# Products of the identity into unused columns of y's bank, ahead of the turning of x in tiles 13 to 23 and ahead of the last logits

## Chip, cores, metric

The kernel runs on one core of one Trainium2 chip. The metric is the device time of one execution in microseconds (us). TensorE is called PE here, VectorE DVE, ScalarE ACT, GpSimd POOL, and SyncE SP.

## What is computed

A recurrent attention (WKV) is followed by a mixture of experts. The shapes are 4 batches, 8 heads, 768 steps, head dimension 48; then 3072 tokens of 384 numbers, 8 experts with an inner width of 1024, each token going to its best two.

```python
for t in range(S):
    cur = np.einsum('bhd,bhe->bhde', u[None] * kt, vt)
    y[:, :, t] = np.einsum('bhd,bhde->bhe', rt, state + cur)
    state = w[None, :, :, None] * state + np.einsum('bhd,bhe->bhde', kt, vt)
...
noisy_logits = x @ w_gate + np.log1p(np.exp(x @ w_noise)) * noise
top2 = np.argpartition(-noisy_logits, 2, axis=1)[:, :2]
...
h = np.maximum(x[mask] @ w1[e], 0.0)
out[mask] += top2_w[mask, k, None] * (h @ w2[e])
```

## The kernel before

**Attention.** The work is cut into 24 tiles of 128 tokens, numbered `i` = 0 to 23 (`i` = 4 x chunk + batch). All instructions of an engine run in the order in which the code writes them; the order around the change is written out by hand in the loop over tiles (L1330 to L1391). For tile `i` the loop does, among other things: `ystate(i)` opens the PSUM bank `py` and multiplies by the carried state (L532); `yout(i)` first takes the logits of tile `i-1` (L574), then the masked scores times v (L532), with the sums for the u term of the next tile in the middle (`uterm_sum`, L434, from tile `PE8` = 13 on); `xout(i)` adds y and the u term on DVE and so makes x (L561); `turn_kr(i+2)` transposes k and r two tiles ahead into the banks `KX` and `RV` (L225), ACT and DVE copy them out as `kT` (L463) and `rT` (L465); `logits_out(i-1)` copies 16 columns of logits out on ACT as `lg` (L583); `scores(i+1)` makes the scores of the next tile in `PAB` (L477), which DVE masks as `am` (L485); and `turn_x(i)` transposes x into `KX` (L225) and has ACT copy it out as `xT` (L471), from which the logits are made one tile later.

**The bank `py`.** Each tile has one PSUM bank of 512 fp32 columns, called `PB[i]`. Columns 0 to 383 hold y, the next 64 hold the logits of the tile before (`PL[i-1]`, which `lg` reads), the next 8, from `CO` = 448, hold the sums of the u term. Columns 456 to 511 are used by nobody.

**The last tile.** For `i` = 23 the loop calls `xT_first` (L1062): it transposes three gathered blocks of tokens for the first expert, two of them into `RV` and `PAB`, then calls its argument, which is `turn_x(23)`, then transposes the third block into `RT` (L1075). ACT rounds the three to `xh` (L1080). `pl_alone(23)` (L1399) makes the last logits (L574, into `pl`), and then the experts begin.

**Experts.** `p1` (L1136) multiplies the blocks by w1 in 9 products of 128x384 for each of 8 slices, writing `ph`; ACT and DVE turn `ph` into `hb`. `p2` (L1172) multiplies `hb` by w2. Routing (the choice of the two experts, lists, gathers) runs in small steps on DVE and POOL between these, from generators that the loops advance.

Of the kernel before, what the change touches and what calls it, by code (L numbers as in the profile page):

```python
# [49 lines left out]
NZ_AT = 5  # L50
CV_DVE = 8
PE8 = 13
GD = 6


@with_exitstack
def kernel(
# [14 lines left out]
    nc = tc.nc  # L72
    B, H, S, D = r.shape
# [99 lines left out]
    def load_nz(b):  # L173
        nc.sync.dma_start(nz[:, :, b, :], noise[b * S:(b + 1) * S, :].rearrange("(c p) e -> p c e", p=128))
# [11 lines left out]
    ident = const.tile([128, 128], F32, name="ident")  # L186
# [35 lines left out]
    def turn_rows(dst, o, src, base=0):  # L222
        for s in range(2):
            q = slice(base + s * 64, base + (s + 1) * 64)
            nc.tensor.transpose(dst[:, s, o:o + 64], src[q], ident[q, q])  # L225
# [4 lines left out]
    def by_row(t):  # L230
        return t.rearrange("p a (s t) -> p s a t", s=2)

    def halves_of(src, o, n):
        return src[:, :, o:o + n * 64].rearrange("p s (a t) -> p s a t", t=64)
# [78 lines left out]
    def consts_b():  # L313
        nc.gpsimd.memset(zrow, 0.0)
# [102 lines left out]
    def uterm_a(i):  # L417
        if i >= PE8:
            t = att.tile([128, 512], F32, name="rku")
            RKU[i] = t.rearrange("p (a t) -> p a t", t=128)  # L420
            for h in (slice(0, NP // 2), slice(NP // 2, NP)):
                nc.gpsimd.tensor_mul(RKU[i][:, h], rT[i][:, h], kT[i][:, h])
            return
        uterm_rk(i)
        uterm_u(i)

    CO = DM + LREP * 2 * E

    def uterm_sum(i, pyb):
        c8 = pyb[:, CO:CO + H].rearrange("p (a s) -> p a s", s=2)  # L430
        for p in range(NP):
            for q in range(2):
                qs = slice(q * 64, (q + 1) * 64)
                nc.tensor.matmul(c8[qs, p, :], RKU[i][:, p, qs], uw[:, p, :], start=False, stop=True,  # L434
                                 skip_group_check=True)
        PC[i] = pyb[:, CO:CO + H]
# [3 lines left out]
    def uterm_b(i):  # L440
        c8 = att.tile([128, H, 1], F32, name="c8", bufs=2)
        if i >= PE8:
            nc.vector.tensor_copy(c8[:, :, 0], PC[i])
# [23 lines left out]
    def turn_x(i):  # L467
        for d in range(ND):
            turn_rows(KX, XO + d * 64, X[i][:, d * 128:(d + 1) * 128])
        XT[i] = att.tile([128, ND, 128], F32, name="xT", bufs=1)  # L470
        nc.scalar.activation(by_row(XT[i]), halves_of(KX, XO, ND), AF.Copy)  # L471

    def scores(i):
        pa = PAB.rearrange("p s (a b) -> p s a b", b=128)
        for p in range(NP):
            for s in range(2):
                nc.tensor.matmul(pa[:, s, p, :], kT[i][s * 64:(s + 1) * 64, p, :],  # L477
                                 rT[i][s * 64:(s + 1) * 64, p, :], start=True, stop=True)
        PA[i] = pa
# [30 lines left out]
    def zup_p(i):  # L510
        if i in ZT:
            nc.gpsimd.tensor_mul(Z[i % B], ZT[i], w128.to_broadcast([128, NP, D]))
# [28 lines left out]
    ACC, PB = {}, {}  # L541

    def yout(i):
        c, b = divmod(i, B)
        py, acc_mm = PY[i], ACC[i]
        if i:
            logits(i - 1, not c)
        for p in range(NP):
            if p == NP // 2 and PE8 <= i + 1 < NT:
                uterm_sum(i + 1, PB[i])  # L550
            for s in range(2):
                h = 2 * p + s
                for q in range(2):
                    acc_mm(py[:, h, :], AM[i][:, s, p, :], vt[i][:, h, :], q, h == H - 1)

    def xout(i):
        c, b = divmod(i, B)
        py = PY[i]
        xr = xs[i % 4]
        x = xr[:, :DM]  # L560
        nc.vector.tensor_add(x, py.rearrange("p h d -> p (h d)"), CV[i].rearrange("p h d -> p (h d)"))  # L561
        X[i] = x

    def xstore(i):
        if i >= 0:
            nc.sync.dma_start(xd[i * 128:(i + 1) * 128, :], xs[i % 4])
# [3 lines left out]
    def logits(i, alone):  # L570
        for d in range(ND):
            for q in range(2):
                qs = slice(q * 64, (q + 1) * 64)
                nc.tensor.matmul(PL[i][qs], XT[i][:, d, qs], wg[:, d, None, :].to_broadcast([128, LREP, 2 * E]),  # L574
                                 start=alone and d == 0, stop=(d == ND - 1), skip_group_check=True)
# [98 lines left out]
    def drop(g, mm2, ej2, ijv, w_, c0, first):  # L674
# [6 lines left out]
        c = 0.1 + 0.004 * wp_  # L681
        n = GD
        parts = []
# [331 lines left out]
    def chunks(e):  # L1015
        return CHUNKS1 if e else CHUNKS0
# [4 lines left out]
    def xgather(e, ci, early_=-1):  # L1021
        for t in chunks(e)[ci]:
            n = tw(t)
            xg = moe.tile([128, XW], F32, name="xg", bufs=4)
            nc.gpsimd.indirect_dma_start(  # L1025
                out=xg[:n, :XW if e else DM], out_offset=None, in_=xd[:rows_of(early_)],
                in_offset=bass.IndirectOffsetOnAxis(ap=GR[:n, e * NJ + t:e * NJ + t + 1], axis=0))
            XG[e, t] = xg
# [33 lines left out]
    def xT_first(between):  # L1062
        xh = moe.tile([128, ND, WMAX], F32R, name="xh")
        xl = moe.tile([128, ND, WMAX], F32R, name="xl")
        XH[0, 0] = (xh, xl)
        part = lambda x, t: by_row(x[:, :, t * 128:(t + 1) * 128])
        whole = RT[:, :ND * 128].rearrange("p (d t) -> p d t", d=ND)
        ts = []
        for t, dst in zip(chunks(0)[0], (RV, PAB, None)):
            if dst is None:  # L1070
                between()
            for d in range(ND):
                xg = XG[0, t][:, d * 128:(d + 1) * 128]
                if dst is None:
                    nc.tensor.transpose(whole[:, d, :], xg, ident)  # L1075
                else:
                    turn_rows(dst, d * 64, xg)
            ts.append((t, whole, xh[:, :, t * 128:(t + 1) * 128], xl[:, :, t * 128:(t + 1) * 128]) if dst is None else
                      (t, halves_of(dst, 0, ND), part(xh, t), part(xl, t)))
            nc.scalar.activation(ts[-1][2], ts[-1][1], AF.Copy)  # L1080
        for t, x, h_, l_ in ts:
            nc.vector.tensor_sub(l_, x, h_.bitcast(F32))
# [161 lines left out]
    def steps(n):  # L1244
        for _ in range(n):
            one_step()
# [67 lines left out]
    def products(i):  # L1314
        if PE8 <= i + 1 < NT:
            uterm_a(i + 1)
        if i + 2 < NT:
            prep_k(i + 2)
        zup_p(i - 1)
        if i + 1 < min(PE8, NT):  # L1320
            uterm_a(i + 1)
# [8 lines left out]
    for i in range(NT):  # L1330
        products(i)
        if early_done and (0, 0) not in XG:
            xgather(0, 0, 0)
        if i + 5 < NT:
            load(i + 5, (0, 2))
        if NZ_AT <= i < NZ_AT + B:
            load_nz(i - NZ_AT)
        if i == B:
            consts_b()
        ystate(i)  # L1340
        if i:
            kvup(i)
        yout(i)
        if not i:
            kvup(i)
        if i + 4 < NT:
            load(i + 4, (2, 3))
        xstore(i - 1)
        zup_v(i)
        if i > 1:  # L1350
            zblock(i - 2)
        uterm_c(i, CV_EARLY, H)
        steps(2)
        tick()
        if CV_DVE < i + 1 < NT:
            uterm_b(i + 1)
        steps(1)
        xout(i)
        while i == I_EARLY and not early_done:
            rstep(1)  # L1360
            maybe_early()
        if i == I_EARLY and (0, 0) not in XG:
            xgather(0, 0, 0)
        if i == NT - 1:
            logits_out(i - 1)
            route_when_done(i - 1)
            xstore(i)
            steps(3)
            xT_first(lambda: turn_x(i))
            p1a = p1(0, 0)  # L1370
        else:
            turn_kr(i + 2)
            if i:
                logits_out(i - 1)
                route_when_done(i - 1)
            uterm_c(i + 1, 0, CV_EARLY)
            steps(1)
            scores(i + 1)
            turn_x(i)
            tick()  # L1380
            steps(1)
            mask(i + 1)
            if i + 1 <= CV_DVE:
                uterm_b(i + 1)
            steps(3)
            maybe_early()
        if i == 5:
            consts_v()
        for p, t in enumerate(W_AT0):
            if W_LD.get(i) == p or t <= i <= t + 2:  # L1390
                next(wun[p])  # L1391
# [273 lines left out]
```

## Time and profile before

| | us |
|---|---|
| median of 3 runs | 592.07 |
| the runs | 592.11, 589.45, 592.07 |
| profiled execution | 594.45 |
| its span, first to last instruction | 592.3 |
| PE busy in the span | 570.7 (96%) |
| DVE, ACT, POOL busy | 346.8, 284.8, 282.0 |

The profile is of one execution, which took 594.45 us: 592.3 us of span and 2.1 us around it. Times inside the profile count from the start of the span. The first expert product starts at 127.65 us, so the attention with its last tile is a bit over a fifth of the span. In the profile, the granted clock of PE is given as a share of full speed: 1.00 is 2.4 GHz and 0.50 is 1.2 GHz, its two levels.

### The profile page before, as it was taken

How to read it: one execution, taken by the hardware profiler on the slowest of the kernel's cores; microseconds unless marked ns; L12 is line 12 of the kernel's file. 1: busy time of each engine (PE TensorE's matmuls, PEld its weight loads, DVE VectorE, ACT ScalarE, POOL GpSimd, SP SyncE). 2: the span in 40 equal slices, each digit the busy share in tenths (PEclk: the TensorE clock that was granted, in tenths of full speed). 3: DMA queues.
4: the chain of work that ended last, by engine and by line, in shares of the span. 5: the costliest groups of instructions: out<-in, count | busy, mean ns of one | idle time of the engine just before them, and what ended most of it. 6: DMA issues, size and time to landing. Idle time of an engine off the chain costs nothing.

```text
span 592.3 us, 13907 instructions
## 1 busy us (share of the span) xinstructions
PE 570.7 (96%) x5383; PEld 544.7 (92%) x5384; DVE 346.8 (59%) x781; ACT 284.8 (48%) x714; POOL 282.0 (48%) x420
## 2 busy tenths in 40 slices
PE   8999989979979999999999999999999999999995
PEld 5899979869979999999999999999999999999995
DVE  7988889778745444546455645555464546454331
ACT  4348877832343443554445554455454454445220
POOL 8997767720426443436345443444353436333222
PEclk9999999989989999999999999999999999999998
DMA  8998999167504643675655646455756555424211
GB/s 162 196 210 190 232 224 233 54 168 225 157 2 140 208 145 92 177 181 146 122 166 142 191 107 185 120 178 111 177 132 152 150 149 171 128 92 85 66 35 42
DMA packets 143225, 86.53 MB, mean 146 GB/s; under 512 B 118624, under 2 KB 133215, under 8 KB 143152
## 3 DMA queue, kind: packets, MB, share of 16 engines
q1 hardware_dynamic: 132368, 56.76, 40.2%
q0 software_dynamic: 10160, 28.81, 16.3%
q8 instruction: 44, 0.72, 0.5%
q14 instruction: 29, 0.24, 0.1%
q10 hardware_dynamic: 624, 0.00, 0.1%
HBM read 58.81 MB, written 19.86 MB: 133 GB/s over the span
## 4 chain that ended last, share of the span: by engine, by line
PE 80%; DVE 7%; POOL 6%; issue 3%; ACT 2%; DMA 1%; another core or an unknown queue 1%; POOLq 0%; DVEq 0%; ACTq 0%
PE ph L1136 36%; PE pym L1172 33%; POOL kd L403 2%; PE pym L1165 2%; PE pym L1163 2%; POOL rku L411 2%; PE py L532 2%; DVE am L485 1%; POOL rku L415 1%; PE PAB L477 1%; DVE x L561 1%; PE KX L225 1%; DVE rT L465 1%; PE RT L714 1%; PE ptm L1054 1%
## 5 line engine op out<-in xcount | busy, mean ns | idle before, releaser
L1172 PE MATMUL pym<-w1h,hb 128*128 128x384 f32 x768 | 200.2, 337 | 0.0
L1142 DVE SCALAR_TENSOR_TENSOR hb<-ph,hb 128x384 fp32r<-128x384 f32 x128 | 71.2, 557 | 119.7 <-ACT ht L1140 73.6
L1172 PEld LDWEIGHTS pym<-w1h,hb 128*128 128x128 f32 x768 | 139.4, 188 | 0.2
L1136 PE MATMUL ph<-xh,w0h 128*128 128x384 f32 (+1 forms) x384 | 136.3, 355 | 0.0
L1136 PE MATMUL ph<-xh,w0l 128*128 128x384 f32 (+1 forms) x384 | 136.2, 355 | 0.0
L1136 PE MATMUL ph<-xl,w0h 128*128 128x384 f32 (+1 forms) x384 | 130.6, 354 | 0.0
L1172 PE MATMUL pym<-w1l,hb 128*128 128x384 f32 x384 | 129.2, 336 | 0.0
L1140 ACT ACTIVATE hb<-ph 128x384 fp32r<-128x384 f32 x128 | 62.9, 492 | 111.2 <-PE ph L1136 106.4
L1197 POOL DMA_INDIRECT out_dram<-ot,TK x56 | 60.0, 1071 | 100.4 <-DVE ot L1191 44.4
L1025 POOL DMA_INDIRECT xg<-xd,GR x56 | 60.9, 1088 | 53.6 <-DVE r_e L608 24.6
L1136 PEld LDWEIGHTS ph<-xh,w0h 128*128 128x128 f32 x384 | 72.9, 190 | 3.7 <-issue 0.2
L1136 PEld LDWEIGHTS ph<-xl,w0h 128*128 128x128 f32 x384 | 72.8, 190 | 3.3
L1136 PEld LDWEIGHTS ph<-xh,w0l 128*128 128x128 f32 x384 | 72.9, 190 | 3.2
L1040 POOL DMA_INDIRECT pv<-out_dram,GA x49 | 50.1, 1022 | 51.0 <-DMA out_dram<-ot,TK 38.6
L1172 PEld LDWEIGHTS pym<-w1l,hb 128*128 128x128 f32 x384 | 72.1, 188 | 0.1
L1110 ACT ACTIVATE xh<-xj 128x384 fp32r<-128x384 f32 (+1 forms) x42 | 21.2, 504 | 43.7 <-DVE xj L1108 38.3
L1180 ACT ACTIVATE ot<-pym 128x384 f32<-128x384 f32 x42 | 20.5, 487 | 41.3 <-PE pym L1172 31.7
L1111 DVE TENSOR_TENSOR xl<-xj,xh 128x384 fp32r<-128x384 f32 (+1 forms) x42 | 22.4, 534 | 24.9 <-ACT xh L1110 18.4
L1096 ACT ACTIVATE pl<-xg 128x768 uint16<-128x768 uint16 (+1 forms) x42 | 35.3, 841 | 1.6 <-DMA xd<-pl 1.5
L485 DVE TENSOR_TENSOR am<-PAB,mneg 128x512 int32<-128x512 int32 x48 | 30.8, 685 | 4.2 <-PE PAB L477 2.8
L454 ACT ACTIVATE cv<-vt,c 128x48 f32<-128x48 f32 x120 | 30.3, 326 | 0.2
L403 POOL TENSOR_TENSOR kd<-kt,tabk 128x192 f32<-128x192 f32 x46 | 28.6, 643 | 3.6 <-PE RV L225 2.4
(275 smaller groups left out, 828.2 us busy)
## 6 DMA issues: line engine op xcount, KB each, us to landing
stg<-in_moe_w_dram SPq DMA_DIRECT2D x24, 512.0 KB
stg<-in_moe_w_dram SPq DMA_DIRECT2D x32, 384.0 KB
xd<-x SPq DMA_DIRECT2D x24, 196.0 KB
rd<-in_r_dram SPq DMA_DIRECT2D x24, 192.0 KB
vt<-in_v_dram SPq DMA_DIRECT2D x24, 192.0 KB
out_dram<-ot SPq DMA_DIRECT2D x16, 288.0 KB
kt<-in_k_dram SPq DMA_DIRECT2D x23, 192.0 KB
xg<-xd,GR POOLq DMA_INDIRECT x56
```

The costliest lines, as they stand in the source:

```text
L403: nc.gpsimd.tensor_mul(KD[i][:, h], kt[i][:, h], tabk[:, h, :D])
L454: nc.scalar.activation(CV[i][:, h, :], vt[i][:, h, :], AF.Copy, scale=C8[i][:, h, :])
L485: nc.vector.tensor_tensor(am[:, :, h].bitcast(I32), pa[:, :, h].bitcast(I32), mneg[:, None].to_broadcast([128, 2, NP // 2, 128]), op=ALU.b ...
L1025: nc.gpsimd.indirect_dma_start(out=xg[:n, :XW if e else DM], out_offset=None, in_=xd[:rows_of(early_)], in_offset=bass.IndirectOffsetOnAxi ...
L1040: nc.gpsimd.indirect_dma_start(out=pv[:n], out_offset=None, in_=out, in_offset=bass.IndirectOffsetOnAxis(ap=GA[:n, e * NJ + t:e * NJ + t + ...
L1096: nc.scalar.activation(pl[:n], XG[e, t][:n, :DM].bitcast(U16).rearrange("p (d two) -> p two d", two=2), AF.Copy)
L1111: nc.vector.tensor_sub(xl, xj, xh.bitcast(F32))
L1136: nc.tensor.matmul(ph[:, :w_], a[:, d, fs], x[:, d, :w_], start=(j == 0), stop=(j == len(q) - 1))
L1140: nc.scalar.activation(h_[:, f, 0, :], ph[:, a:b], AF.Relu)
L1142: nc.vector.scalar_tensor_tensor(h_[:, f, 1, :], ph[:, a:b], 0.0, h_[:, f, 0, :].bitcast(F32), op0=ALU.max, op1=ALU.subtract)
L1172: nc.tensor.matmul(py, hb[:, f, a, hs], x[:, f, :], start=(j == 0), stop=(j == len(q) - 1))
L1197: st = nc.gpsimd.indirect_dma_start(out=out, out_offset=bass.IndirectOffsetOnAxis(ap=TK[:n, q:q + 1], axis=0), in_=ot[:n], in_offset=None, ...
```

## The change

A new function `fill(i, n)` issues `n` fp32 products with the 128x128 identity `ident` as weights and its first 56 columns as the moving operand; they write the 56 unused columns of `PB[i]`. Nobody reads them. Three fills stand ahead of `turn_x(i)` for `i` = 13 to 22, nine ahead of `turn_x(23)` and five behind it, ahead of the last block's transposes and the last logits: 44 in all.

```diff
+FILLS = (3, 9, 5)
...
+    def fill(i, n):
+        t = PB[i][:, CO + H:]
+        for _ in range(n):
+            nc.tensor.matmul(t, ident, ident[:, :t.shape[1]], start=True, stop=True, skip_group_check=True)
+
...
-            xT_first(lambda: turn_x(i))
+            xT_first(lambda: (fill(i, FILLS[1]), turn_x(i), fill(i, FILLS[2])))
             p1a = p1(0, 0)
...
             scores(i + 1)
+            if i >= PE8:
+                fill(i, FILLS[0])
             turn_x(i)
```

The line numbers of the changed file are larger by 1 from `FILLS` on and by 6 from `fill` on. On the other engines the order of instructions is the same as before.

The order on PE at tile 13 (`x_147` is its x), with the engines that each first instruction waits for, before. `DVE` stands there for x, `Activation` for an earlier instruction of ACT.

```order
L477 MATMUL PAB<-rT,kT 128x128 x8
L225 MATMUL KX<-ident,x_147 128x64 [waits DVE_49,Activation_49]
L225 MATMUL KX<-ident,x_147 128x64 x5
L532 MATMUL py<-zb_220,rT 64x96 [waits PE_49,Activation_49]
L532 MATMUL py<-zb_220,rT 64x96 x7
L495 MATMUL RV<-vt,kd_101 48x48 [waits DMAHW3_49,DVE_49]
```

And the same place now.

```order
L478 MATMUL PAB<-rT,kT 128x128 x8
L560 MATMUL py<-ident 128x56 [waits Activation_49]
L560 MATMUL py<-ident 128x56 x2
L226 MATMUL KX<-ident,x_147 128x64 x6
L533 MATMUL py<-zb_220,rT 64x96 [waits PE_49]
L533 MATMUL py<-zb_220,rT 64x96 x7
```

Three fills came in between the scores and the turning of x. The wait moved from the turning to the first fill, names ACT alone, and the turning itself waits for nothing more.

The order on PE in the last tile, before; `xg` are the gathered blocks, `x_149` is x of tile 23.

```order
L225 MATMUL PAB<-ident,xg 128x64 x5
L225 MATMUL KX<-ident,x_149 128x64 [waits DVE_49]
L225 MATMUL KX<-ident,x_149 128x64 x5
L1075 MATMUL RT<-ident,xg 128x128 [waits DMASW2_49]
L1075 MATMUL RT<-ident,xg 128x128 x2
L574 MATMUL pl<-wg,xT 64x64 [waits Activation_49]
```

And now.

```order
L226 MATMUL PAB<-ident,xg 128x64 x5
L560 MATMUL py<-ident 128x56 [waits Activation_49]
L560 MATMUL py<-ident 128x56 x8
L226 MATMUL KX<-ident,x_149 128x64 x6
L560 MATMUL py<-ident 128x56 x5
L1081 MATMUL RT<-ident,xg 128x128 [waits DMASW2_49]
L1081 MATMUL RT<-ident,xg 128x128 x2
L580 MATMUL pl<-wg,xT 64x64 [waits Activation_49]
```

Nine fills moved in ahead of the turning of the last x and took over its wait, and five stand between it and the third block.

## Rows read from the trace of the kernel before

**Rows 1.** The page, busy us of each engine, share of the span, instructions
```profile
PE 570.7 (96%) x5383; PEld 544.7 (92%) x5384; DVE 346.8 (59%) x781; ACT 284.8 (48%) x714; POOL 282.0 (48%) x420
```

**Rows 2.** Busy us by stretch, then PE's clock, DMA share, GB/s
```profile
124.60:128.00 3.40, 1.81 (x27) 1.35 (x24) 3.10 (x9) 1.89 (x6) 0.00 (x0) 1.00 0.35 70
128.00:131.40 3.40, 3.40 (x13) 3.40 (x12) 2.12 (x12) 0.51 (x2) 0.00 (x0) 0.50 0.99 272
131.40:134.80 3.40, 3.40 (x21) 3.40 (x20) 3.13 (x10) 0.99 (x2) 0.00 (x0) 0.99 0.93 290
...
169.00:172.40 3.40, 3.02 (x18) 2.81 (x18) 1.57 (x5) 1.91 (x4) 0.00 (x0) 0.50 0.00 0
```

**Rows 3.** Chain that ended last: start us, us, engine, tile, line
```profile
81.98 0.48 DVE x L561
82.59 0.40 PE KX L225 x6
...
86.37 1.71 issue
...
94.47 0.40 PE KX L225 x6
...
107.74 1.43 POOL kd L403 x2
109.21 0.34 PE KX L225 x4
...
122.01 1.29 DVE am L485 x2
...
127.72 14.38 PE ph L1136 x72
...
210.32 4.17 PE pym L1172 x24
```

**Rows 4.** Timeline, PE turning x: start us, us, instruction, [idle before]
```profile
82.59 0.40 PE L225 MATMUL KX<-ident,x 64*128 64x64 f32 x6 [0.57 <-DVE x L561]
...
94.47 0.40 PE L225 MATMUL KX<-ident,x 64*128 64x64 f32 x6 [0.31 <-DVE x L561]
...
105.69 0.40 PE L225 MATMUL KX<-ident,x 64*128 64x64 f32 x6 [0.61 <-DVE x L561]
...
120.46 0.40 PE L225 MATMUL KX<-ident,x 64*128 64x64 f32 x6 [1.13 <-DVE x L561]
...
125.79 0.40 PE L225 MATMUL KX<-ident,x 64*128 64x64 f32 x6 [1.10 <-DVE x L561]
```

**Rows 5.** Timeline, ACT copying the logits out in the same tiles
```profile
82.48 0.18 ACT L583 ACTIVATE lg<-py 128x16 f32<-128x16 f32 x1 [1.01 <-DVE x L561]
...
94.36 0.18 ACT L583 ACTIVATE lg<-py 128x16 f32<-128x16 f32 x1 [0.81 <-DVE x L561]
...
120.50 0.18 ACT L583 ACTIVATE lg<-py 128x16 f32<-128x16 f32 x1 [2.73 <-DVE x L561]
...
125.77 0.18 ACT L583 ACTIVATE lg<-py 128x16 f32<-128x16 f32 x1 [1.59 <-DVE x L561]
```

**Rows 6.** Line L583, 60 to 130 us: ACT idle before it, us, times
```profile
  DVE x L561: 8.6, 8
```

**Rows 7.** PE by line and shape, 124.6 to 127.66 us: busy us, mean ns
```profile
L574 PE MATMUL pl<-wg,xT 128*64 128x64 f32 x12 | 0.6, 230 | 0.5 <-ACT xT L471 0.5
```

**Rows 8.** Timeline of the last tile, PE and ACT
```profile
126.12 0.55 PE L1075 MATMUL RT<-ident,xg 128*128 128x128 f32 x3
...
126.59 0.51 ACT L471 ACTIVATE xT<-KX 128x384 f32<-128x384 f32 x1
...
126.96 0.52 ACT L1080 ACTIVATE xh<-RT 128x384 fp32r<-128x384 f32 x1
...
127.15 0.57 PE L574 MATMUL pl<-wg,xT 128*64 128x64 f32 x12 [0.49 <-ACT xT L471]
...
127.65 0.44 PE L1136 MATMUL ph<-xh,w0h 128*128 128x384 f32 x1
```

## Prediction

> **What bounds the kernel now.** I read the busy times first, then the clock by stretches, the chain of waits, and the timeline around each turning of x. PE is busy for 570.7 of 592.3 us [rows 1], so most of the kernel is a queue of products, and a change pays if it shortens that queue, raises its clock, or removes a wait ahead of it. The expert stage after 127.65 us is nearly all PE; there the clock counts. It falls to half (1.2 GHz) twice before the end: at 128.0 to 131.4 us, right as the expert products begin, and at 169.0 to 172.4 us [rows 2]. In the stretch ahead of the first fall, 124.6 to 128.0, PE was busy for 1.81 of 3.40 us [rows 2]. The second fall lies 40 us behind the last fill, and the change does nothing there.
>
> Inside the attention, from tile 13 on, the chain goes back and forth between DVE, POOL and PE [rows 3]. PE stands idle ahead of turning x in five of the eleven tiles that the change touches (15, 17, 19, 22 and 23), for 0.57, 0.31, 0.61, 1.13 and 1.10 us, each time until DVE has made x [rows 4]. In the other six tiles x is there before PE asks for it.
>
> **What the fills wait for.** The fills stand ahead of the turning, where PE waits for x, and the first thing to settle is whether they can run in that wait. The two orders say no: the first fill waits for ACT, and behind it the turning waits for nothing, though it needs x. So ACT's instruction must itself come behind x. It is `lg`, which reads columns of the same bank `py`; where ACT is early, `lg` sits idle until DVE is done with x, 8 times for 8.6 us [rows 6]. The rows of the five tiles agree: `lg` starts 0.03 to 0.1 us behind the end of x and takes 0.18 [rows 5]. The fills therefore start behind x *and* behind `lg`; the old idle time stays as it was, and the fills come on top.
>
> The Trainium skill has a rule for this ("PSUM — Partial Sum Buffer", section "PSUM bank collisions raise a hardware error"): guard PSUM by bank, not by address, since two engines may not be in one bank's partitions at a time even in different columns. The waits of `lg` for x agree with it, and it speaks against this change: unused columns of a bank in use are no free place. By columns alone the fills of tiles 15, 17, 19 and 22 would lie in the idle time and cost nothing; by the rule they cost what follows.
>
> **Price of a fill.** The trace has no such product. A fill is an fp32 product with 128 columns of weights and 56 moving ones. The nearest row is the last logits: 12 records, run as two halves side by side, take 0.57 us at a mean of 230 ns [rows 7, 8], so the last pair starts 0.34 us behind the first, 5 steps of 0.068. A product is two steps there (6 products, 12 records), so 0.14 a fill from above. From below, three transposes of 128 columns take 0.55 us [rows 8] with a last one of about 0.3, so 0.13 a record; 56 of 128 columns are 0.057, twice that 0.11. I take 0.12: 0.36 for three, 1.08 for nine, 0.60 for five. At half clock each is twice as long.
>
> **Tiles 13, 14, 16, 18.** PE does not wait for x, DVE is the chain (x to x, as at 81.98 us [rows 3]), and the 0.36 that PE loses is taken back at the next wait for x, 0.57, 0.31 and 0.61 us [rows 4]. On the chain: 0. Without that cover it would be 0.36 each.
>
> **Tiles 15 and 17.** The chain passes from x to PE here (82.59 and 94.47 [rows 3]). `lg` ends at 82.66 and 94.54 [rows 5], PE follows some 0.06 later as it follows x now, so the turning starts 0.13 + 0.36 = 0.49 us later in each. Behind tile 15 stands a gap of 1.71 us for which the profile names no cause [rows 3]; if its end is fixed, the first 0.49 disappears in it, so I count half: 0.25 + 0.49 = 0.74.
>
> **Tiles 19 to 22.** In 19 PE loses 0.49 too, but the chain goes from x over `rT` and POOL's products to the turning of k at 109.21 [rows 3], where PE had waited 0.13 for POOL: 0.36. In 20 and 21 PE is the chain without a wait: 2 x 0.36 = 0.72. In 22 the turning would be 0.28 + 0.36 = 0.64 later; PE waits 1 us for `xT` behind it, and the mask that the chain takes next starts at 122.01, 1.15 us behind the last turning [rows 3, 4]. I count 0, up to 0.64. PE also waits for its own last fill ahead of the state product in each tile, 0 to 0.05 us.
>
> Tiles 13 to 22 together: 0.74 + 0.36 + 0.72 = 1.82 us, between 1.4 and 2.7.
>
> **Tile 23.** `lg` ends at 125.95 [rows 5], nine fills take PE to 127.08, the turning of x to about 127.35 instead of 126.05. Five fills run to 127.95 while ACT makes `xT`; that hides them from the logits but not from the third block, whose transposes now end at 127.95 + 0.55 = 128.5. Its rounding on ACT takes 0.52 [rows 8], and the first expert product needs it: 129.1 in place of 127.65, 1.45 us later. In before that rounding lay under the logits. If fills cost 0.11, it is 1.3; with 0.14, 1.75.
>
> **The clock.** From 126.0 us PE would run with little pause up to the experts, where the row of before has 1.81 of 3.40 us busy [rows 2]. If the clock then stays at 2.4 GHz, the 72 products of the first `p1` take 72 x 4.17 / 24 = 12.5 us in place of 14.38 [rows 3]: 1.9 us back. (Half of the 3.4 us at half clock is 1.7, about the same.)
>
> **Sum.** +1.82 + 1.45 - 1.9 = +1.4 us on the profiled 594.45, so 595.8 there. The three runs are 592.11, 589.45 and 592.07; the profiled one lies 2.4 above their median. On the median: 593.4.
>
> **Rivals.**
> *The clock falls all the same.* The idle time ahead of 126.0 grows by 0.2 us rather than shrinking, so the fall can come anyway, perhaps sooner, with the fills themselves at half speed; or it is absent already from some runs of before, as the one at 589.45 may show. Then nothing is given back: +1.82 + 1.45 = +3.3, 595.4, and up to 596.5 with the upper prices. For it: the waits of 1.13, 1.01 and 1.10 us remain. Against it: the waits at 82 to 106 us are of 0.3 to 0.6 us with a gap of 1.71, and there the clock stayed up.
>
> *Faster: the delays are covered and the clock holds.* The place is the start of `p1`. If the delays of tiles 15 to 21 vanish in waits that the profile names badly (the 1.71 us gap, POOL ahead of 109.21), some 0.5 remains, and with 1.3 in the last tile and 1.9 back the sum is about -0.1 to -0.5, 591.8. If the new count of PE instructions also moves or dissolves that 1.71 us gap, -2.0: 590. It decides below a cost of 1.9 us for all fills together, against 3.3 in my sum. By the Trainium skill ("TensorE: Matmul & The Clock Gate", Part 1) "the default state is throttled, and activity releases the throttle", so fills of any content would do; the trace shows one fall behind a half-idle stretch, in agreement. By that rule alone, without the waits, the sum would be the 1.9 us gain.
>
> *The change does not do what it says.* The fills were to stand in the wait for x. Should they not wait for `lg` after all, they would lie in the five waits: 0.72 for tiles 20 and 21, some 0.5 in the last tile, 1.9 back: -0.7, 591.4. The orders speak against it.
>
> **How the numbers follow.** Forecast (waits as derived, clock holds) 0.50, 592.4 to 594.6; clock falls all the same 0.27; delays covered 0.16; fills not behind `lg` 0.07. The likeliest is 593.4. The range reaches to 590.2, the covered case with the gap moved, and to 596.3, the fallen clock with upper prices. About 0.5% is what a measurement of this kernel can tell from no change: below 589.1 is faster, above 595.0 slower. Faster takes the far part of the covered cases (0.11); slower takes most of the fallen clock and a little of the forecast's upper end (0.23); the same, 0.66.
>
> **What would show it.** In the changed profile: fills at L560 that start behind `lg` of the same tile, with idle time ahead of them ended by ACT `lg` of about 0.6 to 1.4 us in tiles 15, 17, 19, 22 and 23; steps of about 0.06 us for each record; the first expert product at about 131 us; no half clock behind it, and the first 72 products in 12.5 us. Wrong would be: fills that begin before x ends, a half clock at the first expert products (then slower), or a first expert product before 129.5 us (then faster).

## The result, and the profile after

| | before | after |
|---|---|---|
| median, us | 592.81 (19 runs, 589.45 to 598.23) | 599.17 (19 runs, 593.71 to 601.19) |
| ratio to before, 95% interval | 1 | 1.0096 [1.0074, 1.0119] |
| profiled execution, us | 594.45 | 597.32 |
| its span, us | 592.3 | 595.3 |

The change made the kernel slower by about 1%, 5.7 us by the ratio. The forecast was 593.4 (590.2 to 596.3) with "same" as the likeliest; the time lies above the range.

The page of after: the span, then busy us of each engine with share and instructions, then the chain that ended last by engine.

```profile
span 595.3 us, 14065 instructions
...
PE 581.2 (98%) x5471; PEld 554.9 (93%) x5472; DVE 348.0 (58%) x781; ACT 284.5 (48%) x714; POOL 280.0 (47%) x420
...
PE 90%; DVE 3%; POOL 2%; SPq 1%; issue 1%; ACT 1%; DMA 1%; POOLq 0%; DVEq 0%; ACTq 0%
```

Against [rows 1] PE has 88 more instructions (44 fills of two records each) and 10.5 us more busy time; the other engines are as before. The sum had given the 44 fills 44 x 0.12 = 5.3 us.

The stretch from the end of x of tile 12 to the end of x of tile 23, in before and then in after (columns as in [rows 2]). It holds the same work in both, and in after the 60 records of the fills of ten tiles besides.

```profile
65.80:125.74 59.94, 52.82 (x1359) 49.54 (x1355) 49.37 (x131) 43.58 (x150) 42.05 (x59) 1.00 0.69 171
```

```profile
67.11:128.39 61.28, 60.30 (x1419) 56.72 (x1415) 50.29 (x131) 43.30 (x150) 42.02 (x59) 1.00 0.70 171
```

PE is busy for 7.5 us more, and its idle time falls from 7.1 us to 1.0: it has hardly any slack left. The chain of after in tiles 15 to 17 (start us, us, engine, tile, line) says the same; where [rows 3] change between DVE, POOL and PE, there is only PE:

```profile
85.18 0.80 PE py L560 x6
85.98 0.33 PE KX L226 x6
86.32 0.81 PE py L533 x16
...
89.88 0.95 PE PAB L478 x16
90.83 0.81 PE py L560 x6
91.63 0.33 PE KX L226 x6
...
95.52 0.50 PE PAB L478 x7
```

Three fills (6 records) hold PE for 0.80 us, 0.27 each. Then the last tile, PE's timeline (start us, us, line, instruction, [idle before]), and ACT's `lg` and `xh` from the same stretch:

```profile
128.66 2.25 PE L560 MATMUL py<-ident 128*128 128x56 f32 x18 [0.73 <-ACT lg L589]
130.84 0.58 PE L226 MATMUL KX<-ident,x 64*128 64x64 f32 x6
131.36 2.38 PE L560 MATMUL py<-ident 128*128 128x56 f32 x10
133.53 0.86 PE L1081 MATMUL RT<-ident,xg 128*128 128x128 f32 x3
134.32 0.91 PE L580 MATMUL pl<-wg,xT 128*64 128x64 f32 x12
135.16 0.69 PE L1142 MATMUL ph<-xh,w0h 128*128 128x384 f32 x1
```

```profile
128.42 0.18 ACT L589 ACTIVATE lg<-py 128x16 f32<-128x16 f32 x1 [1.02 <-DVE x L567]
...
134.43 0.49 ACT L1086 ACTIVATE xh<-RT 128x384 fp32r<-128x384 f32 x1 [2.41 <-PE RT L1081]
```

The nine fills start behind `lg`, as foretold. Ten records of the second group take longer than eighteen of the first: the clock has fallen in between. By windows (PE, PEld, DVE, ACT, POOL busy, then the clock):

```profile
124.60:128.00 3.40, 3.33 (x82) 2.98 (x80) 3.23 (x9) 2.13 (x8) 2.50 (x3) 1.00 0.60 164
128.00:131.40 3.40, 2.74 (x25) 2.53 (x25) 1.93 (x5) 0.95 (x3) 0.00 (x0) 0.90 0.48 103
131.40:134.80 3.40, 3.40 (x23) 3.07 (x23) 0.00 (x0) 0.86 (x2) 0.00 (x0) 0.50 1.00 299
134.80:138.20 3.40, 3.40 (x20) 3.28 (x18) 2.46 (x11) 0.34 (x3) 0.00 (x0) 0.60 0.99 304
...
169.00:172.40 3.40, 3.40 (x18) 3.14 (x17) 2.61 (x8) 2.84 (x7) 2.50 (x3) 1.00 0.24 87
```

By these shares the half clock runs from about 130.7 to 137.5 us, 6.8 us, against 3.4 in [rows 2], and most of the last tile lies in it. The second fall of [rows 2] is absent here.

**An account by stretches.** The table cuts the profiled span of every kernel at three places: the end of x of tile 12 (the first fill is in tile 13), the end of x of tile 23, and the start of the first expert product; beside them stands the length of the first 72 expert products in the chain. In after, for one, x of tile 23 is the row below, which ends at 128.39, and the first expert product is at 135.16, 6.77 later.

```profile
127.83 0.56 DVE L567 TENSOR_TENSOR x<-py,cv 128x384 f32<-128x384 f32 x1
```

| kernel | x(12) ends | x(12) to x(23) | x(23) to first expert product | from there to the end | first 72 products |
|---|---|---|---|---|---|
| before | 65.80 | 59.93 | 1.92 | 464.6 | 14.38 |
| after | 67.11 | 61.28 | 6.77 | 460.1 | 13.91 |
| after_again | 68.41 | 60.56 | 6.64 | 460.2 | 14.13 |
| e1_tiles | 69.76 | 64.67 | 1.91 | 460.8 | 12.96 |
| e2_last | 66.89 | 59.18 | 7.85 | 464.4 | 14.43 |
| e3_halves | 66.86 | 61.45 | 3.65 | 464.6 | 12.95 |
| e4_kx | 66.55 | 62.82 | 4.21 | 459.8 | 12.95 |
| e5_kx_halves | 68.33 | 62.29 | 3.05 | 459.2 | 13.16 |
| e6_bf16 | 68.91 | 57.67 | 2.47 | 460.5 | 14.02 |
| e7_waits | 70.86 | 58.44 | 1.92 | 459.1 | 12.97 |
| e8_bf16_kx | 67.11 | 58.73 | 2.26 | 460.5 | not in its chain |
| e9_bf16_kx_more | 66.41 | 59.48 | 1.91 | 459.1 | 12.95 |

Inside the second stretch the time from one x to the next, by the tile that the later x belongs to (starts of the rows of x), shows where the tiles differ:

| kernel | 13 | 14 | 15 | 16 | 17 | 18 | 19 | 20 | 21 | 22 | 23 |
|---|---|---|---|---|---|---|---|---|---|---|---|
| before | 5.07 | 5.54 | 6.04 | 4.51 | 7.38 | 5.23 | 5.98 | 4.20 | 4.81 | 5.85 | 5.33 |
| after | 5.17 | 6.53 | 6.01 | 5.27 | 5.72 | 5.98 | 6.02 | 5.05 | 5.49 | 5.40 | 4.64 |
| e1_tiles | 4.91 | 5.60 | 6.03 | 5.26 | 5.72 | 5.98 | 6.02 | 5.05 | 5.49 | 8.26 | 6.35 |
| e3_halves | 5.06 | 6.29 | 6.04 | 4.92 | 5.73 | 5.35 | 6.02 | 4.62 | 5.17 | 8.25 | 4.01 |
| e4_kx | 5.06 | 6.04 | 6.03 | 5.26 | 5.72 | 5.98 | 6.00 | 5.07 | 5.49 | 8.25 | 3.91 |

Tile 17 of before and tile 22 of three others stand out, and neither is the work of the fills. In before tile 17 holds the pause of 1.71 us for which the profile names no cause ([rows 3]); in the other eleven profiles the same tile takes 5.70 to 5.73. In e1_tiles, e3_halves and e4_kx tile 22 takes 2.85 us longer than in after. Up to there e1_tiles has the same instructions as after, so the fills alone don't make it. The products of PE come there with pauses (`issue`, where PE waits for nothing that the profile shows) or more slowly, 16 products for the scores in 1.94 us and in e3_halves in 2.36, in place of 1.11. The rows of e4_kx:

```profile
122.25 0.43 PE L533 MATMUL py<-vt,am 128*64 128x48 f32 x6 [0.37 <-issue]
122.98 0.30 PE L533 MATMUL py<-vt,am 128*64 128x48 f32 x2 [0.31 <-issue]
123.22 1.94 PE L478 MATMUL PAB<-rT,kT 64*128 64x128 f32 x16
```

So the column from x(12) to x(23) contains 1.7 us in before, and some 2.9 us in these three, that another execution need not have.

Two more columns differ for reasons that are not the change. Up to x of tile 12 all twelve programs have the same order, and yet single executions lie between 65.8 and 70.9 (those of 68.4 and more mostly have a half clock at 63 to 69 us). Behind the first expert product, three of them (before, e2_last, e3_halves) are some 4 to 5 us longer than the others: PE waits there once for 2.8 to 3.5 us, and a half clock follows, as at 169 us in [rows 2]. In before it is

```profile
169.38 1.16 PE L714 MATMUL RT<-r_ob,r_oa 128*128 128x100 bf16 x12 [2.85 <-ACT r_ob L705]
```

In e1_tiles the wait is 2.08 us and no half clock follows; the other eight profiles have no wait over 1 us there. So the span of before that was profiled contains some 4 us which a further execution need not have. That is why the two profiled spans differ by only 3.0 us. What the change itself touches is +1.35 (tiles 13 to 23) + 4.85 (last tile) - 0.47 (first 72 products) = +5.7 us, as much as the ratio gives; single profiles are good to a microsecond or two, so the agreement is closer than can be asked for; without the pause in tile 17 of before the first term would be +3.0.

### The profile page after: what moved, and what is told of

It is laid out like the page before. It is cut to its first block, busy times and chain, and to the rows that moved or that the text cites. A ratio compares the mean times of both kernels' runs of the same rounds, so it can differ in the third digit from the quotient of the medians.

```text
span 595.3 us, 14065 instructions
## 1 busy us (share of the span) xinstructions
PE 581.2 (98%) x5471; PEld 554.9 (93%) x5472; DVE 348.0 (58%) x781; ACT 284.5 (48%) x714; POOL 280.0 (47%) x420
## 4 chain that ended last, share of the span: by engine, by line
PE 90%; DVE 3%; POOL 2%; SPq 1%; issue 1%; ACT 1%; DMA 1%; POOLq 0%; DVEq 0%; ACTq 0%
PE ph L1142 36%; PE pym L1178 33%; PE py L533 4%; PE PAB L478 3%; PE py L560 2%; PE KX L226 2%; PE pym L1171 2%; PE pym L1169 2%; SPq L158 1%; PE py L580 1%; PE RV L226 1%; PE py L435 1%; DMA kt<-in_k_dram 1%; PE RV L496 1%; PE RT L720 1%
## 5 line engine op out<-in xcount | busy, mean ns | idle before, releaser
L1031 POOL DMA_INDIRECT xg<-xd,GR x56 | 59.5, 1063 | 52.3 <-DVE r_e L614 28.4
```

What stands on the lines that cost most here:

```text
L1031: nc.gpsimd.indirect_dma_start(out=xg[:n, :XW if e else DM], out_offset=None, in_=xd[:rows_of(early_)], in_offset=bass.IndirectOffsetOnAxi ...
```

## Experiments

Each is an edit of the changed kernel. A fill "behind `lg`" writes the bank of y as in the change; one "in KX" writes unused columns of the bank that the turning of x itself writes.

**The fills of the tiles alone, and those of the last tile alone.**

```diff
-FILLS = (3, 9, 5)
+FILLS = (3, 0, 0)      # e1_tiles
+FILLS = (0, 9, 5)      # e2_last
```

> Only the three fills of tiles 13 to 22 stay; the nine and five of the last tile are left out. Price theory: a fill takes 0.29 us (0.87 for three in the trace of the changed kernel, against 0.36 forecast), 8.7 us of PE in ten tiles, of which the 4 to 6 us that PE waited there before take up most: x of tile 23 is ready 2 to 3.5 us later than before, the last tile is as before with half clock at the first expert products, and the whole is 2 to 3.5 us slower than before. Rival, the last tile carries the loss: within 1 us of before.

Measured: 599.93 us (597.09 to 605.56, 10 runs) against 595.34 of before on this chip, 1.0104 [1.0066, 1.0142].

> Only the nine and five fills of the last tile stay; those of tiles 13 to 22 are left out. Price theory: 14 fills take 3.1 us at 2.4 GHz (0.22 each when in a row) and up to 6 at 1.2 GHz, so the first expert product starts 3.5 to 6 us later than before; if the clock is then full there, 1.9 comes back: 2 to 4.5 us slower than before. Rival, my forecast's price of 0.12: 1.45 later and 1.9 back, 0.5 us faster than before.

Measured: 601.71 us (600.31 to 605.88, 4 runs), 1.0124 [1.0059, 1.0188].

Both lost more than any theory expected. Each half of the change costs about as much as the whole, so the two don't add, and no run settles why; the mean granted clock is 0.989 in e1_tiles and 0.983 in e2_last (four runs only), 0.991 in before. In the profile of e1_tiles two things make the stretch of the tiles long (64.67 in the table). One is tile 22 with its pauses, which e3_halves and e4_kx have at full clock as well. The other is half clock, from 126.2 to 133.1 us; it is over ahead of the expert products, whose first 72 then take 12.96. In e2_last nothing but the last tile has changed, and the clock falls during the nine fills and stays down longest of all:

```profile
126.34 3.33 PE L560 MATMUL py<-ident 128*128 128x56 f32 x18 [1.32 <-ACT lg L589]
...
130.12 2.38 PE L560 MATMUL py<-ident 128*128 128x56 f32 x10
```

```profile
124.60:128.00 3.40, 2.08 (x24) 1.95 (x22) 2.88 (x10) 0.95 (x3) 0.00 (x0) 0.88 0.27 65
128.00:131.40 3.40, 3.40 (x20) 3.18 (x21) 0.00 (x0) 0.49 (x1) 0.00 (x0) 0.50 1.00 263
131.40:134.80 3.40, 3.40 (x24) 2.95 (x24) 1.01 (x3) 0.67 (x2) 0.00 (x0) 0.50 0.77 228
134.80:138.20 3.40, 3.40 (x14) 3.40 (x13) 1.86 (x10) 0.49 (x1) 0.00 (x0) 0.61 1.02 315
```

Here PE waits 1.32 us for x and `lg`, and then the fills, though PE is busy with them without a pause from 126.34 on, run into half clock. From x of tile 23 to the first expert product it takes 7.85 us in place of 1.92. The fills that were to save the clock are at half speed themselves.

**The price: the same fill as two products of 64 weight columns.**

```diff
-            nc.tensor.matmul(t, ident, ident[:, :t.shape[1]], start=True, stop=True, ...)
+            for q in (slice(0, 64), slice(64, 128)):
+                nc.tensor.matmul(t[q], ident[:, q], ident[:, :t.shape[1]], start=True, stop=True, ...)
```

> Each fill is cut into two products of 64 columns of weights, the form of the logits, from which I had taken the price; places and waits are as in the changed kernel. Price theory (a full-width product this short does not load its weights under the one before): a fill falls to about 0.12 to 0.14 us, tiles 13 to 22 cost 1.5 to 2.5 us, the last tile 1.5 to 2, and if the clock holds 1.9 come back: 1 to 3 us slower than before, 3 to 5 faster than the changed kernel. Rival, the wait for the copy of the logits is what costs: no faster than the changed kernel by over 1 us.

Measured: 598.46 us (596.01 to 601.13, 10 runs), 1.0051 [1.002, 1.0083].

```profile
124.63 0.56 PE L561 MATMUL py<-ident 128*64 128x56 f32 x12 [1.69 <-ACT lg L591]
125.12 0.40 PE L226 MATMUL KX<-ident,x 64*128 64x64 f32 x6
...
128.59 1.26 PE L561 MATMUL py<-ident 128*64 128x56 f32 x36 [0.41 <-ACT lg L591]
129.78 0.40 PE L226 MATMUL KX<-ident,x 64*128 64x64 f32 x6
```

From start to start, nine fills hold PE for 1.19 us, 0.13 each, and three for 0.49, 0.16 each. So the price of the forecast, 0.12, is about that of a fill in halves, which is where it had been read ([rows 7]), and not that of the fill in the change. With less work some idle time behind x and `lg` is back in the last tile (0.41), as the forecast had it for the change; the 1.69 stands in tile 22, behind the pauses told above. The kernel is still slower than before, by 3.0 us, the upper end of the price theory's 1 to 3; under the changed kernel it is by the ratios 2.7 us, less than that theory's 3 to 5 and more than the 1 of its rival.

**The wait: the same fills in KX,** where they wait neither for `lg` nor for x. The five behind the turning stay in y's bank.

```diff
-    def fill(i, n):
-        t = PB[i][:, CO + H:]
+    def fill(i, n, kx=True):
+        t = KX[:, 0, XO + ND * 64:XO + ND * 64 + 56] if kx else PB[i][:, CO + H:]
...
-            xT_first(lambda: (fill(i, FILLS[1]), turn_x(i), fill(i, FILLS[2])))
+            xT_first(lambda: (fill(i, FILLS[1]), turn_x(i), fill(i, FILLS[2], False)))
```

> The fills ahead of turning x write 56 unused columns of the bank KX instead of y's, so they need not wait for x and the copy of the logits; the five behind the last turning stay where they are. Wait theory (the bank of y is what costs): the fills vanish in PE's waits for x, and the kernel is within 1 us of before. Price theory: 0.87 us in each tile is more than PE waited for x in most of them, so tiles 13 to 22 cost nearly as much as in the changed kernel, the last tile 1 to 2 us less: 3 to 5 us slower than before.

Measured: 596.12 us (594.34 to 600.98, 10 runs), 1.0016 [0.9983, 1.005].

```profile
128.87 2.21 PE L560 MATMUL KX<-ident 128*128 128x56 f32 x18
131.01 0.40 PE L226 MATMUL KX<-ident,x 64*128 64x64 f32 x6
131.34 1.32 PE L560 MATMUL py<-ident 128*128 128x56 f32 x10
132.50 0.50 PE L1081 MATMUL RT<-ident,xg 128*128 128x128 f32 x3
...
133.58 0.44 PE L1142 MATMUL ph<-xh,w0h 128*128 128x384 f32 x1
```

Here is the price at full clock: nine fills 2.14 us from start to start, 0.24 each, five 1.16, 0.23 each. No idle time stands ahead of them, the profile is at full clock throughout these stretches, and the first 72 products take 12.95 us. The mean granted clock of its runs is 0.996, that of before on the same chip 0.991. The full-price work is still there, the clock pays for it, and nothing is left of the loss that can be measured (the interval reaches to 0.5%, 3 us). So the price theory's 3 to 5 us did not come, and the wait theory's "within 1 us" came for another reason than it gave: the fills did not vanish in the waits, as the numbers of the next run show.

**The changed kernel again,** on a second chip with the three that follow.

> The changed kernel as it is, beside the others on one chip, so that its time splits into work at the full clock and what the granted clock takes. The share of the clock lost over the span costs about its part of the span: 0.983 to 0.998 in the runs of before went with 599 to 592 us. Both theories expect 4 to 7 us over before. Work theory: 3 to 4.5 of it are there at equal clock. Clock theory: at equal clock the two kernels are within 1.5 us, and the changed one is granted less.

Measured: 598.42 us (594.55 to 601.18, 12 runs) against 593.27, 1.0072 [1.0039, 1.0105]. The loss is there again, with half clock from about 131.6 to 138.4 us. Its runs fall in two groups by the granted clock: four at 0.998 or 0.999 take 594.6 to 595.2 us, eight at 0.985 to 0.991 take 597.1 to 601.2. The 19 runs of the first series do the same (six at 0.997 to 0.999: 593.7 to 595.5; thirteen at 0.985 to 0.991: 597.3 to 601.2). In a third of its executions the clock stays near full, and even there it is not below the median of before.

The two theories can be told apart by these numbers. The mean granted clock of the changed kernel is 0.992 here and that of before 0.990, so the change is not granted less, and the clock theory fails. At 0.995 and above the changed kernel takes 595.1 us (median of four runs) and before 591.5 (two runs); on its own chip e4_kx takes 595.5 at such clocks (eight runs) and before 591.9 (five). So at near-full clock about 3.6 us of work are left, in whichever bank the fills ahead of the turning stand, within the 3 to 4.5 of the work theory. What goes with the bank is how often the clock holds: 8 of the 10 runs of e4_kx are at 0.995 or more, 10 of the 31 of the changed kernel, and 7 of the 60 of before on these two chips.

**Cheap and in the wait: halves in KX.** The two edits above together.

> Both remedies at once: fills ahead of turning x write the bank KX, and each fill is two products of 64 columns of weights. Work theory: 0.16 us a fill, 0.5 in a tile, of which the waits for x take a part: work 1 to 2.5 us over before. Clock theory: the fills stand in the waits, the clock is granted 0.995 or more as with KX alone, which gives back 2 to 3 us: in all -1 to +1 us against before.

Measured: 592.74 us (590.27 to 595.89, 12 runs), 0.9984 [0.9954, 1.0014]; mean clock 0.997, before 0.990. That is what the clock theory expected, with the work of the halves paid by the clock.

**The places and waits of the change without its work:** each fill is one bf16 product (of zeros), in y's bank behind `lg`.

```diff
-            nc.tensor.matmul(t, ident, ident[:, :t.shape[1]], start=True, stop=True, ...)
+            nc.tensor.matmul(t, wsrc, wsrc[:, :t.shape[1]], start=True, stop=True, ...)
```

> Places, waits and counts of the changed kernel, but each fill is one bf16 product of zeros, 0.05 to 0.06 us in place of 0.27. If the work of the fills is what costs, the work goes back to within 1 us of before. If the wait behind the copy of the logits costs by itself (0.13 us a tile that waits for x, and the wait for the last fill ahead of the state product), 1 to 2 us of work stay. The clock, with so little in the fills, is no better than before: 0.5 to 2 us slower than before in all.

Measured: 591.69 us (590.94 to 593.92, 12 runs), 0.9975 [0.995, 1.0].

```profile
126.85 0.39 PE L560 MATMUL py<-wsrc 128*128 128x56 bf16 x9 [2.04 <-ACT lg L589]
127.17 0.40 PE L226 MATMUL KX<-ident,x 64*128 64x64 f32 x6
```

Nine such fills hold PE for 0.32 us, 0.036 each. They wait for `lg` exactly as those of the change, 2.04 us here, and the kernel is not slower, against 0.5 to 2 us expected. The wait for `lg` itself costs nothing that can be seen, and without the work of the fills the loss is gone (mean clock 0.993, before 0.990). The half clock at the expert products is as in before (first 72 products 14.02 us).

**Fills in halves in idle places only:** five in KX in tile 22, six in KX ahead of the last turning, five and two in y's banks ahead of the last two logits, none elsewhere.

```diff
+        if i == NT - 1:
+            fill(i, 5, False, False)
         if i:
             logits(i - 1, not c)
...
-            xT_first(lambda: (fill(i, FILLS[1]), turn_x(i), fill(i, FILLS[2])))
+            xT_first(lambda: (fill(i, 6), turn_x(i)))
+            fill(i, 2, False)
...
-            if i >= PE8:
-                fill(i, FILLS[0])
+            if i == NT - 2:
+                fill(i, 5)
```

> A version meant to be faster: fills of two products of 64 columns of weights only where PE was idle at the end of the attention in the trace of before, and in places that wait for nothing new: five in KX ahead of the turning of x in tile 22, five in y's bank ahead of the logits in tile 23, six in KX ahead of the last turning, two ahead of the last logits. Clock theory: the clock is granted 0.994 or more in place of 0.990, at 0 to 0.7 us of work: 1 to 3 us faster than before. Work theory: no gain, 0 to 1 us slower.

Measured: 592.05 us (589.94 to 594.5, 12 runs), 0.9979 [0.9952, 1.0007]; mean clock 0.993. In its profile the clock holds at the first expert products (12.97 us for 72). Whether it is faster by the 1 to 3 us of the clock theory these runs cannot tell.

**Bf16 fills in KX, with the counts of the change and with more,** on a third chip, an attempt at a version better than both.

```diff
+FILLS = (3, 9, 5)      # e8_bf16_kx, fills as in e6_bf16, places as in e4_kx
+FILLS = (9, 18, 6)     # e9_bf16_kx_more
```

> The places and counts of the change, each fill one bf16 product of zeros (0.187 us with its end, short steps, as the bf16 fills of the run before showed), and the fills ahead of the turning of x write unused columns of KX, so they wait neither for lg nor for x; the five of the last tile stay in y's bank. Theory (work on PE decides, and fills that stand in the wait keep the clock up): work as before within 0.5 us, clock .996 or more, no half clock at the first expert products, 0.4 to 0.7% faster than before (ratio 0.993 to 0.996). Rival (the clock follows how long PE is really busy, and bf16 fills are too short to matter in the wait): clock as before, .990, half clock at the first expert products as before, ratio 0.998 to 1.001.

Measured: 589.88 us (588.79 to 591.31, 12 runs) against 591.3, 0.9981 [0.996, 1.0001]; mean clock 0.994, before 0.991.

> As the kernel next to it, with 9 instead of 3 bf16 fills in each of tiles 13 to 22, 18 instead of 9 and 6 instead of 5 in the last tile. Theory: 6 more fills at a step of about 0.03 us are 0.18 us per tile; hidden in the wait in tiles 15, 17, 19, 22, 23 and paid in at most five others, so at most +0.9 us of work against its neighbour, with the clock as high or higher: ratio 0.994 to 0.998. Rival (any fill pushes PE into the chain): +1.8 us and more against its neighbour, ratio over 0.998.

Measured: 591.01 us (588.15 to 592.87, 12 runs), 0.9993 [0.9968, 1.0018]; mean clock 0.995.

The theory was too hopeful for both. The ratio of e8_bf16_kx is the one that its rival expected, with a clock between the two; e9_bf16_kx_more is 1.1 us over its neighbour, between its theory (0.9 at most) and its rival (1.8). The clock rises a little, and the 0.1 to 0.2% by which the time falls these runs cannot tell from none. In the profile of e8_bf16_kx PE has 1.76 us idle between its fills and the turning, and the half clock still comes:

```profile
123.73 0.41 PE L560 MATMUL KX<-wsrc 128*128 128x56 bf16 x9
125.90 0.40 PE L226 MATMUL KX<-ident,x 64*128 64x64 f32 x6 [1.76 <-DVE x L567]
```

Of all versions none beats the kernel before beyond its interval; five (e5 to e9) lie 0.07 to 0.25% under it.

## Why the prediction was wrong

**Wrong: the price of a fill.** This is the step that failed first of all. 0.12 us was forecast, from 0.11 to 0.14; it is 0.23 to 0.24 in long groups and 0.27 in the groups of three (e4_kx, after). The lower bound, "56 of 128 columns are 0.057", scaled a step with the moving columns, and the upper one came from products of 64 weight columns that run as two halves side by side. A full-width fill has 128 weight columns and only 56 moving ones. Its 18 records take 2.21 us in e4_kx, (2.14 / 18) 0.12 each, about what the transposes with 128 moving columns take at the same width, so the step doesn't fall with the moving columns here. e3_halves shows the difference in one edit: 0.13 for the same result in halves. So the upper bound, read from halves, was no bound.

The Trainium skill has a rule that bears on this step ("TensorE: Matmul & The Clock Gate", Part 3, section "The mechanism"): a weight load runs beside products in flight only when it goes to other rows of the array. By it load and product of full-width fills take turns, and the 0.12 a record fits. The halves of e3_halves don't fit: they too go to the same rows (they differ in columns), and yet they ran side by side. So the runs show that a fill costs about half when its weights are cut to 64 columns, and the reason stays open. By its section "LDWEIGHTS (loading the stationary operand)", 128 columns take 128 / 1.2 = 107 ns, and an estimate from that, 2 x (107 + 23) with the 23 ns of 56 columns at 2.4 GHz, would have been 0.26 a fill. The load records themselves last 186 to 192 ns in e4_kx and overlap, so they don't show the 107.

**Right in size by luck: tiles 13 to 22.** +1.82 (1.4 to 2.7) was forecast up to x of tile 23; measured +1.35 in after, and +0.63 in after_again. The pause of before in tile 17 hides 1.7 of the loss: without it after lost 3.0. The five kernels with cheap fills there or few of them (e2_last, e6_bf16 to e9_bf16_kx_more) took 57.7 to 59.5 us, by which after lost 1.8 to 3.6. Which tiles pay was largely foretold. The fills of tile `i` count between x of `i` and x of the next tile: by the table of tiles those of 14, 16 and 18 cost nothing, as forecast, and those of 15, 17, 19 and 20 cost 0.76, 0.75, 0.85 and 0.68, nearly the whole of three fills (0.81). Those of 13, taken at nothing, cost about as much (0.99, with pauses of 0.51 us in after and 0.33 in before), and with those of 21 and 22 the time to the next x fell by 0.45 and 0.69, where PE of before had waited for x and `xT`. In all 7.5 us of added work met some 4.4 us of idle time (6.1 less the pause), which it used up, and in after PE is the chain through all these tiles.

**Wrong: the last tile.** +1.45 was forecast; +4.85 came (x to first expert product 6.77 in place of 1.92). At full clock it would have been 0.27 (from x to the end of `lg`, and 0.06) + 2.14 + 2.57 (from the turning to the first expert product, in e4_kx) = 4.98, that is +3.06: the price alone makes +1.6 of the miss. The other 1.79 is half clock.

**Wrong: the clock.** 1.9 us were to come back; 0.47 did. The first 72 products at full clock take 12.95 us (e4_kx, e9_bf16_kx_more), not 12.5, which was the rate of the products of `p2`, so there were 1.43 to win; and in both profiles of the change the clock fell all the same, now ahead of the experts (a third of the runs kept it near full). The rival "the clock falls all the same" named this, with the fills at half speed, at 0.27 and with a loss of 3.3; at the measured prices its own sum would be 3.8 for the tiles and 3.1 for the last tile, an estimate of 6.9 against the 5.7 measured. By that estimate the price adds 3.6 us to the forecast, and the clock that was not given back 1.9. The row that spoke for it was the idle time ahead of the last turning, which the change could not shorten.

**Right:** the first fill waits for `lg`, which waits for x, and so fills don't stand in the wait. The profile has this in the last tile (0.73 us) and in e2_last, e3_halves and e6_bf16; where the fills went to KX instead it was gone. The Trainium skill's rule of guarding PSUM by bank ("PSUM — Partial Sum Buffer", section "PSUM bank collisions raise a hardware error") agrees with these waits. Their cost, though, was put too high (0.13 a tile): e6_bf16 has them all and is not slower.

**What stays open.** What decides whether the clock falls in the last tile is not settled. In the profiles the idle time directly ahead of the fills or the turning there is 0.73, 0.73, 1.32, 2.04, 1.76 and (before) 1.10 us where it fell in or behind the last tile, and 0, 0, 0.34, 0.41 and 1.22 where it didn't (e4, e5, e7, e3, e9). (e1_tiles, whose fall came and was over ahead of it, is left out.) That goes together but for the last, and is one profile each. Nor is it shown what the pauses in tile 17 of before and in tile 22 of three others come from.

## What to carry to other kernels

Price a filler product by its weights as well as by its moving columns, and from a row with the same width of weights; a bound read from products that run as halves side by side is none. Idle time on an engine covers added work only until it is used up, so set the sum of the added work against the sum of the idle time in the stretch (here 7.5 us against some 4.4) and leave out pauses that another execution need not have. A filler that shall keep the clock up should stand in the wait itself: look at which bank it writes and who reads that bank, for behind the wait it was mostly work here. And even a filler that keeps the clock is worth it only if it costs less than the clock gives back: e4_kx held the clock and was no faster than before.

## What was not expected of the hardware

A busy PE did not keep its clock: in e2_last PE ran fills without a pause from 126.34 us and the clock went to half about 0.9 us later; in after it fell 2.0 us behind the start of the nine. Here the Trainium skill's sentence that activity releases the throttle ("TensorE: Matmul & The Clock Gate", Part 1) does not tell the moment: the fall came in the middle of the activity, behind the idle time, and fills that stood in the wait instead went with a higher mean clock (0.996 and 0.997 in e4_kx and e5_kx_halves; 0.992 in the changed kernel, 0.983 in the four runs of e2_last).

A bf16 fill holds PE for 0.036 us, an fp32 fill of the same 128 by 56 columns for 0.24, nearly seven times as much; the fp32 one is two records, and its weight-load records take 186 to 192 ns each against 95 ns:

```profile
L560 PEld LDWEIGHTS <-wsrc x44: 95/95/99, 74.6 to 127.6; 128*128 128x128 bf16 x44
```

```profile
L560 PEld LDWEIGHTS KX<-ident x78: 186/192/192, 72.7 to 130.8; 128*128 128x128 f32 x78
```

(The view is that of line L560 in e6_bf16 and in e4_kx; the durations are minimum, median and maximum in ns.)
